# State times weight in two heads: 64-row tiles on half the array each, in place of operands stacked over 128 rows

## The chip, the core and the metric

The kernel runs on one core of a Trainium2 chip. The metric is the device time of one execution in microseconds (us), the median of several runs. The core's engines are TensorE (PE, with its weight loads as PEld), VectorE (DVE), ScalarE (ACT), GpSimd (POOL) and SyncE (SP), which issues all the DMAs here. Each runs its own instructions in order and waits for the others by semaphores.

## The reference

Eight batches of eight heads: `x` is 512 x 64 per head, `state` 32 x 64. Attention is run in both directions, and the result goes through two gated products (d_model 512, d_ff 1536).

```python
scores = scale * np.matmul(x, state.transpose(0, 1, 3, 2))
a = softmax(scores)
xread = np.matmul(a, state)
scores2 = scale * np.matmul(state, x.transpose(0, 1, 3, 2))
a2 = softmax(scores2)
sread = np.matmul(a2, x)
attn = np.concatenate([xread, sread], axis=2)
...
h = attn @ moe_w_a * (attn @ moe_w_b) @ moe_w_out
g = h @ moe2_w_gate
out = (g * sigmoid(g) * (h @ moe2_w_val)) @ moe2_w_out
```

`softmax` stands here for the lines that subtract the maximum, exponentiate and divide; the last lines are the bodies of two functions. The weights come as 64-bit numbers and are turned into 32-bit ones on the chip.

## The kernel before, in words

For the rows that come from `xread`, `attn @ w` is `a @ (state @ w)`: the kernel multiplies each head's state by the 64 rows of the weight that belong to that head, and the attention weights `a` then take the place of the activations. This product, **state @ w**, is the place of the change. It is made for q = 0, 1 (batches 0 to 3 and 4 to 7, whose four states of 32 rows make the 128 columns of one left operand), for fp = 0 to 5 (512 columns of both first weights) and for eight heads.

Every product is made in a 32-bit format with a shortened mantissa (fp32r). A number is split into a high part, the cast (`copy` on ACT), and a low part, the rest (`subtract` on DVE), and a product of two split numbers is a few matmuls that are summed in a PSUM bank. `convert` makes a 32-bit weight `cv_w` of 128 rows, that is the rows of heads 2p and 2p + 1, by steps on ACT, DVE and POOL. `stacked` (L415) splits it so that for each head h the buffer `w[:, h]` holds the head's high part over its own 64 partitions and its low part over the other 64: two casts (L420) and two subtractions (L336, called for the low parts) over 64 partitions each. The state is laid out twice, over partitions 0 to 63 and again over 64 to 127, and split by `states` into `st_hi` and `st_lo`.

`state_w` (L441) takes one `w` and makes the two heads one after the other. For a head it takes one PSUM bank (tag `pt`) and issues two matmuls over all 128 rows: `st_hi` by the stack (L450), which sums high x high and high x low, and `st_lo` by the stack (L451). `sw_out` copies the bank to `swo` (L328 on ACT or L330 on DVE) and writes it to a tensor in DRAM, from which `sw` later reads `swr` and splits it into `swh` and `swl` for the main product `p` (L652). For q = fp = 0 the copies go straight to the first `swr`.

There are two banks with the tag `pt`; scores (`psc`, `pr`), transposes (`pat`, `pa`, `pst`), the attention product `psr` and the states' products `sw` share them. The main products use the other banks.

The order on all engines is written by a planner before anything runs. Each task has engines it may run on, an estimated cost (`PASS_US` for a matmul of 512 columns), a due time `by` and perhaps a start. `Program.order` hands out, engine by engine, the due task that fits, provided that its buffers (`w`, `h` and the two `pt` banks) are free in the planner's own count; the engines then keep that order. A pool of spare tasks, `warm` (L901, two small matmuls each), fills PE's gaps in the start. Each weight tile is converted, split and multiplied with the state of q = 0; the products with q = 1 are listed after the four tiles of an fp and come due later.

After the first products (p, po, about 700 us) come those of the second layer (pA to pD, pu); the change touches none of them.

Of the kernel before, what the change touches and what calls it, by code (L numbers as in the profile page):

```python
# [10 lines left out]
F32 = mybir.dt.float32  # L11
# [7 lines left out]
P = 128  # L19
# [30 lines left out]
DUE = (-8.0, 12.0, 29.0, -17.0, 92.0, 4.0)  # L50
# [15 lines left out]

ACT_US, DVE_US, FAST_US, POOL_US = ((0.09, 0.84e-3), (0.07, 1.05e-3), (0.07, 0.53e-3), (0.2, 2.6e-3))
PASS_US, HALF_PASS_US = 0.2267, 0.12
HOP_US, PE_HOP_US = 0.25, 0.3
DMA_US, DMA_ISSUE_US, DMA_BYTES_PER_US = 2.2, 0.5, 3.6e5  # L70

# [3 lines left out]
def act(n):  # L75
    return {"ACT": ACT_US[0] + ACT_US[1] * n}


def dve(n, fast=False):
    a, b = FAST_US if fast else DVE_US  # L80
    return {"DVE": a + b * n}
# [176 lines left out]
class Kernel:  # L258
# [151 lines left out]
        self.hi_lo(raw, lambda: raw.t, hi, lambda: hi.t, lo, lambda: lo.t, 1024)  # L410
        return hi, lo

    def stacked(self, name, src_buf, src, **kw):

        nc = self.nc  # L415
        w = self.w_buf(name)
        for h in range(2):
            own, oth = slice(64 * h, 64 * h + 64), slice(64 - 64 * h, 128 - 64 * h)
            self.p.add(
                act(512), lambda e, own=own, h=h: nc.scalar.copy(w.t[own, h], src()[own]), [src_buf], [(w, (h, 0))],  # L420
                **kw
            )
            self.subtract(
                lambda oth=oth, h=h: w.t[oth, h], lambda own=own: src()[own],
                lambda own=own, h=h: w.t[own, h].bitcast(F32), dve(512), [src_buf, (w, (h, 0))], [(w, (h, 1))], **kw
            )
        return w

    def sw_out(self, ps, d, dst, name, by, here=None):

        o = self.h_buf(name)
        self.copy(lambda: o.t, lambda: ps.t, 512, [ps], [o], by=by + 2)
        if here is not None:
            raw, head = here
            r = 32 * (head % 4)
            self.dma(
                lambda: raw.t[r:r + 32, head // 4], lambda: o.t[::4], [o], [(raw, head)], 32 * 2048, by=by + 3
            )
        self.dma(lambda: dst(d.t), lambda: o.t, [o], [(d, name)], P * 2048, by=by + 5)

    def state_w(self, st, fp, p, w, q, by):  # L441

        hi, lo = st
        for h in range(2):
            head = 2 * p + h
            c = slice(head * P, (head + 1) * P)
            ps = self.bank(f"sw{q}_{fp}_{head}")

            def fn(pe, ps=ps, h=h, c=c):
                pe.matmul(ps.t, lhsT=hi.t[:, c], rhs=w.t[:, h], start=True, stop=False)  # L450
                pe.matmul(ps.t, lhsT=lo.t[:, c], rhs=w.t[:, h], start=False, stop=True)  # L451

            self.pe(2 * PASS_US, fn, [hi, lo, (w, (h, 0)), (w, (h, 1))], [ps], by=by)
            r = 32 * (head % 4)
            self.sw_out(
                ps, self.sw_d[q, fp], lambda t, head=head, r=r: t[:, head // 4, r:r + 32].rearrange("b n c -> n b c"), f"swo{q}_{fp}_{head}", by,
                (self.sw_first, head) if q == fp == 0 else None
            )

# [432 lines left out]
    def body(self):  # L892
        nc, p = self.nc, self.p
# [23 lines left out]
        begin, t = {}, FIRST_US  # L917
# [6 lines left out]
        def made(f):  # L924

            return begin[0, f]
# [4 lines left out]
        for fp in range(NFP):  # L931
            t0 = made(2 * fp)
            late = []
            for k in range(KD):
                nm = f"w1_{fp}_{k}"
                t, f = self.convert(self.wab[0][fp, k], nm, by=t0 - DUE[0], start=max(0, t0 - LEAD[0]))
                d = self.wf[fp, k]
                self.dma(lambda d=d: d.t, f, [(t, 0)], [d], P * 2048, by=t0 + 30)
                w = self.stacked(nm, (t, 0), f, by=t0 - DUE[0] + 2)
                self.state_w(st[0], fp, k, w, 0, t0 - DUE[0] + 4)  # L940
                late.append((st[1], fp, k, w, 1, t0 + DUE[1] + 3 * k))
            for a in late:
                self.state_w(*a)
            for f in (2 * fp, 2 * fp + 1):
                wo1[f] = self.weight(self.wo[0][f], f"wo1_{f}", by=begin[0, f] + DUE[2], start=max(0, begin[0, f] - LEAD[1]))
        ws, sw, xs_s = {}, {}, []
        for blk, lo, hi in order:
            self.stretch = STRETCH[0] if blk in range(4) else STRETCH[1]
            t0 = self.clock = max(self.clock, begin[blk, lo])
# [7 lines left out]
            if blk == "s":  # L957
# [14 lines left out]
                xb, n = xs_s, ST  # L972
            else:
# [4 lines left out]
                xb, n = xs[blk], T  # L978
# [18 lines left out]
        for u in range(0, B, 2):  # L997
            ops = self.operands(u, u + 1, self.clock - 30)
            xs_s = []
            if u == B - 2:  # L1000
                d = self.x2["s"]
                for k in range(KD):
# [3 lines left out]
                        start=self.clock - 10  # L1006
# [58 lines left out]
```

## Time and profile before

| | |
|---|---|
| median of 3 runs | 1496.96 us (1496.48 to 1498.74) |
| span of the profiled execution | 1495.1 us; its own time beside that is not listed |
| PE busy, modelled | 1486.0 us, 7016 matmuls |
| DVE, ACT, POOL busy | 1050.2, 648.3, 102.1 us |
| granted clock | 1.000 of full |
| state @ w on PE | 192 matmuls, from 22.9 to 312.9 us |

The span runs from the first to the last instruction. "Busy" on PE counts a matmul from its start to a modelled end, so overlapping ones count once, and short gaps are covered; the distance from one start to the next tells more. In the timeline, a length with a count covers a merged run. Weight loads (PEld) overlap the matmul before them.

### The profile page before, as it was taken

The numbers are of one execution on the slowest core, as the hardware profiler recorded it, in microseconds if no ns is written. First come the engines' busy times: TensorE is split into PE (matmuls) and PEld (weight loads), VectorE is DVE, ScalarE is ACT, GpSimd is POOL, SyncE is SP. The second block draws the span as 40 slices with busy tenths as digits, with TensorE's granted clock in tenths as the row PEclk, the third lists the DMA queues.
The fourth block names the chain that finished last, engine by engine and source line by source line (L and its number), as shares of the span: only waits on it lengthen the run. The fifth ranks groups of instructions, "written<-read, shape, count | busy, mean of one in ns | idle before, by whom it ended". The sixth has DMA issues, their size and how long they took to land.

```text
span 1495.1 us, 19610 instructions
## 1 busy us (share of the span) xinstructions
PE 1486.0 (99%) x7016; PEld 1241.0 (83%) x7016; DVE 1050.2 (70%) x1786; ACT 648.3 (43%) x1152; POOL 102.1 (7%) x78
## 2 busy tenths in 40 slices
PE   9999999999999999999999999999999999999998
PEld 8777888788888888998888888888888888888887
DVE  7999758756787778776777996466855577545554
ACT  7777656644556566655333432222323133222220
POOL 1212102100011111110000100000000000000000
PEclk9999999999999999999999999999999999999999
DMA  8765644744455466666947886355664446433412
GB/s 318 274 243 200 232 181 158 260 155 145 171 202 200 169 244 224 243 227 245 386 172 250 305 317 252 138 188 198 244 234 164 140 183 232 169 112 129 155 57 71
DMA packets 111185, 305.90 MB, mean 205 GB/s; under 512 B 11760, under 2 KB 12784, under 8 KB 111088
## 3 DMA queue, kind: packets, MB, share of 16 engines
q1 hardware_dynamic: 111088, 304.66, 56.8%
q8 instruction: 55, 0.90, 0.2%
q14 instruction: 42, 0.34, 0.1%
HBM read 223.35 MB, written 80.74 MB: 203 GB/s over the span
## 4 chain that ended last, share of the span: by engine, by line
PE 96%; ACT 1%; DVE 1%; DMA 1%; issue 1%; SPq 0%; ACTq 0%; DVEq 0%
PE pu L851 17%; PE p L652 17%; PE po L687 17%; PE pC L757 9%; PE pB L757 9%; PE pA L757 9%; PE pD L757 4%; PE p_s L652 2%; PE psr L612 2%; PE psc L503 1%; PE sw L450 1%; PE sw L451 1%; PE pvs L652 1%; PE po_s L687 1%; PE pgs L652 1%; PE pus L851 1%
## 5 line engine op out<-in xcount | busy, mean ns | idle before, releaser
L687 PE MATMUL po<-hs,wo 128*128 128x512 f32 x1152 | 287.3, 393 | 0.0
L687 PEld LDWEIGHTS po<-hs,wo 128*128 128x128 f32 x1152 | 215.1, 188 | 45.1 <-issue 1.4
L652 PE MATMUL p<-xs,swh 128*128 128x512 f32 x768 | 238.3, 391 | 0.0
L652 PEld LDWEIGHTS p<-xs,swh 128*128 128x128 f32 x768 | 143.3, 188 | 29.7 <-issue 0.5
L652 PE MATMUL p<-xs,swl 128*128 128x512 f32 x384 | 149.6, 390 | 0.0
L757 PE MATMUL pB<-x,w 128*128 128x512 f32 x576 | 146.2, 389 | 0.0
L757 PE MATMUL pA<-x,wg 128*128 128x512 f32 x576 | 146.2, 389 | 0.0
L851 PE MATMUL pu<-wo,hv 128*128 128x512 f32 x576 | 140.6, 389 | 0.0
L851 PE MATMUL pu<-wo,hu 128*128 128x512 f32 x576 | 138.5, 389 | 0.0
L757 PEld LDWEIGHTS pA<-x,wg 128*128 128x128 f32 x576 | 108.1, 188 | 22.4
L757 PEld LDWEIGHTS pB<-x,w 128*128 128x128 f32 x576 | 108.1, 188 | 22.4
L851 PEld LDWEIGHTS pu<-wo,hu 128*128 128x128 f32 x576 | 107.9, 188 | 22.2
L851 PEld LDWEIGHTS pu<-wo,hv 128*128 128x128 f32 x576 | 107.9, 188 | 22.2
L771 DVE TENSOR_TENSOR t<-c,pB 128x512 f32<-128x512 f32 x96 | 65.7, 685 | 82.3 <-PE pB L757 80.4
L671 DVE TENSOR_TENSOR a<-a,p 128x512 f32<-128x512 f32 x96 | 65.7, 684 | 70.5 <-PE p L652 57.6
L775 ACT ACTIVATE av<-t 128x512 f32<-128x512 f32 x48 | 30.3, 632 | 176.4 <-DVE t L771 173.2
L328 ACT COPY a<-p 128x512 f32<-128x512 f32 x87 | 51.0, 586 | 91.2 <-PE p L652 84.6
L343 ACT CAST hs<-a 128x512 fp32r<-128x512 f32 x96 | 59.8, 622 | 62.0 <-DVE a L671 52.4
L652 PEld LDWEIGHTS p<-xs,swl 128*128 128x128 f32 x384 | 72.1, 188 | 15.2
L869 DVE TENSOR_TENSOR part<-part,pu 128x512 f32<-128x512 f32 x64 | 43.7, 684 | 47.8 <-PE pu L851 47.6
L336 DVE TENSOR_TENSOR hs<-a,hs 128x512 fp32r<-128x512 f32 x96 | 69.0, 719 | 11.2 <-ACT hs L343 10.4
L757 PE MATMUL pC<-x,wv 128*128 128x512 f32 x288 | 73.1, 389 | 0.0
(180 smaller groups left out, 2365.7 us busy)
## 6 DMA issues: line engine op xcount, KB each, us to landing
w<-w SPq DMA_DIRECT2D x120, 512.0 KB, 4.9
sw<-swo SPq DMA_DIRECT2D x96, 256.0 KB, 2.8
wg<-w2g SPq DMA_DIRECT2D x48, 512.0 KB, 4.7
wv<-w2v SPq DMA_DIRECT2D x48, 512.0 KB, 4.8
wo<-w2o SPq DMA_DIRECT2D x48, 512.0 KB, 6.0
swr<-sw SPq DMA_DIRECT2D x47, 512.0 KB, 4.9
raw_w<-in_wab SPq DMA_DIRECT2D x24, 512.0 KB, 7.1
xt<-in_xt SPq DMA_DIRECT2D x32, 256.0 KB, 5.0
```

What stands on the lines that cost most here:

```text
L328: self.nc.scalar.copy(out(), in_())
L336: lambda e: self.by_engine[e].tensor_tensor(out=out(), in0=in0(), in1=in1(), op=ALU.subtract), r, w, **kw
L343: self.p.add(act(n), lambda e: self.nc.scalar.copy(hi(), src()), [src_buf], [hb], **kw)
L612: pe.matmul(ps.t[:, :256], lhsT=a2.t[:, l], rhs=xn.t[:, r], start=c == 0, stop=c == 3)
L652: pe.matmul(ps.t[:, :n], lhsT=l, rhs=r, start=i == 0, stop=i == last)
L671: self.vec(n, lambda v, a=a, pb=pb: v.tensor_tensor(out=a.t[:, :n], in0=a.t[:, :n], in1=pb.t[:, :n], op=ALU.mult), [pb], [a])
L687: pe.matmul(ps.t[:, :n], lhsT=wo[f].t[:, hw, c], rhs=hs.t[:, hh, :n], start=st, stop=sp)
L757: pe.matmul(ps.t, lhsT=w.t[:, hw, c], rhs=x.t[:, hx], start=start and i == n == 0, stop=stop and i == 1 and n == 2, skip_group_check=True)
L771: self.vec(512, lambda e: e.tensor_tensor(out=out.t, in0=ta(), in1=tb(), op=op), [a, b], [out])
L775: p.add(act(n), lambda e: nc.scalar.activation(out=a.t[:, :n], in_=g.t[:, :n], func=AF.Sigmoid), [g], [a])
L851: pe.matmul(ps.t, lhsT=h.t[:, hh, c], rhs=wo[f].t[:, hw], start=f == steps[0] and i == 0, stop=f == steps[-1] and i == 2)
L869: self.vec(w, lambda v: v.tensor_tensor(out=to(), in0=part.t[:, j % 2, :w], in1=ps.t[:, :w], op=ALU.add), [ps, (part, j)], [ok], by=by)
```

## The change

`stacked` goes. A weight is split plainly, by `hi_lo`: one cast over 128 rows to `w[:, 0]` and one subtraction to `w[:, 1]`. `state_w` takes both banks at once and issues six matmuls as one task: high x high, high x low and low x high, and in each of the three first the head of partitions 0 to 63, then that of 64 to 127, each reading 64 rows of `lhsT` and `rhs`, and writing its own bank. The product low x low, which the stack brought along, is no longer made. The task costs the planner `3 * PASS_US + SWITCH_US` in place of two tasks of `2 * PASS_US`; `SWITCH_US` is a number for the order alone.

```diff
+SWITCH_US = 0.25
...
-    def stacked(self, name, src_buf, src, **kw):
-
-        nc = self.nc
-        w = self.w_buf(name)
-        for h in range(2):
-            own, oth = slice(64 * h, 64 * h + 64), slice(64 - 64 * h, 128 - 64 * h)
-            self.p.add(
-                act(512), lambda e, own=own, h=h: nc.scalar.copy(w.t[own, h], src()[own]), [src_buf], [(w, (h, 0))],
-                **kw
-            )
-            self.subtract(
-                lambda oth=oth, h=h: w.t[oth, h], lambda own=own: src()[own],
-                lambda own=own, h=h: w.t[own, h].bitcast(F32), dve(512), [src_buf, (w, (h, 0))], [(w, (h, 1))], **kw
-            )
-        return w
...
     def state_w(self, st, fp, p, w, q, by):
 
         hi, lo = st
+        ps = [self.bank(f"sw{q}_{fp}_{2 * p + h}") for h in range(2)]
+
+        def fn(pe):
+            for n, (l, k) in enumerate(((hi, 0), (hi, 1), (lo, 0))):
+                for h in range(2):
+                    rows, c = slice(64 * h, 64 * h + 64), slice((2 * p + h) * P, (2 * p + h + 1) * P)
+                    pe.matmul(ps[h].t, lhsT=l.t[rows, c], rhs=w.t[rows, k], start=n == 0, stop=n == 2)
+
+        self.pe(3 * PASS_US + SWITCH_US, fn, [hi, lo, w], ps, by=by)
         for h in range(2):
             head = 2 * p + h
-            c = slice(head * P, (head + 1) * P)
-            ps = self.bank(f"sw{q}_{fp}_{head}")
-
-            def fn(pe, ps=ps, h=h, c=c):
-                pe.matmul(ps.t, lhsT=hi.t[:, c], rhs=w.t[:, h], start=True, stop=False)
-                pe.matmul(ps.t, lhsT=lo.t[:, c], rhs=w.t[:, h], start=False, stop=True)
-
-            self.pe(2 * PASS_US, fn, [hi, lo, (w, (h, 0)), (w, (h, 1))], [ps], by=by)
...
-                ps, self.sw_d[q, fp], lambda t, head=head, r=r: t[:, head // 4, r:r + 32].rearrange("b n c -> n b c"), f"swo{q}_{fp}_{head}", by,
+                ps[h], self.sw_d[q, fp], lambda t, head=head, r=r: t[:, head // 4, r:r + 32].rearrange("b n c -> n b c"), f"swo{q}_{fp}_{head}", by,
...
-                w = self.stacked(nm, (t, 0), f, by=t0 - DUE[0] + 2)
+                w = self.w_buf(nm)
+                self.hi_lo(
+                    (t, 0), f, w, lambda w=w: w.t[:, 0], w, lambda w=w: w.t[:, 1], 512, by=t0 - DUE[0] + 2
+                )
```

With other tasks the planner writes another order, from the first state @ w on. Names below are buffers: `sw_0_6` is the bank of fp 0, head 6; the number behind it tells buffers of one name apart; `x2` counts equal instructions. Line numbers have moved: L336 and L330 are L337 and L331 after the change, L652 and L687 are L638 and L673.

First place: PE in the start, from heads 6 and 7 of the first weights, before:

```order
L450 MATMUL sw_0_6_329<-w_0_3_255,st_hi 128x512
L451 MATMUL sw_0_6_329<-w_0_3_255,st_lo 128x512
L901 MATMUL warm<-ident 128x128 x4
L450 MATMUL sw_0_7_346<-w_0_3_255,st_hi 128x512
L451 MATMUL sw_0_7_346<-w_0_3_255,st_lo 128x512
L567 MATMUL pat_0_352<-ident,sn_0_116 128x128 x4
L901 MATMUL warm<-ident 128x128 x4
L567 MATMUL pat_1_374<-ident,sn_1_152 128x128 x4
```

and after, where the same two heads stand:

```order
L503 MATMUL pr_1_415<-strt_118,xt_1_0_361 128x128
L503 MATMUL pr_1_415<-strt_118,xt_1_1_366 128x128
L489 MATMUL psc_1_427<-xt_1_0_361,strt_118 128x512
L489 MATMUL psc_1_427<-xt_1_1_366,strt_118 128x512
L887 MATMUL warm<-ident 128x128 x6
L435 MATMUL sw_0_6_453<-w_0_3_254,st_hi 128x512
L435 MATMUL sw_0_7_454<-w_0_3_254,st_hi 128x512
```

Heads 6 and 7 have moved behind block 0's transposes `pat` and behind block 1's scores `pr` and `psc`, which stood after them.

Second place: DVE in the start, at the low parts of the first four weights, before:

```order
L330 COPY sT_0_237<-psc_0_202 128x512
L336 TENSOR_TENSOR w_0_0_166<-cv_w_0_0_104,w_0_0_166 64x512 x2
L336 TENSOR_TENSOR w_0_1_210<-cv_w_0_1_134,w_0_1_210 64x512 x2
L336 TENSOR_TENSOR w_0_2_222<-cv_w_0_2_148,w_0_2_222 64x512 x2
L336 TENSOR_TENSOR w_0_3_255<-cv_w_0_3_154,w_0_3_255 64x512 x2
L330 COPY swo_0_4_313<-sw_0_4_304 128x512
```

and after:

```order
L331 COPY sT_0_237<-psc_0_201 128x512
L337 TENSOR_TENSOR w_0_0_166<-cv_w_0_0_104,w_0_0_166 128x512
L337 TENSOR_TENSOR w_0_1_209<-cv_w_0_1_134,w_0_1_209 128x512
L337 TENSOR_TENSOR w_0_2_221<-cv_w_0_2_148,w_0_2_221 128x512
L337 TENSOR_TENSOR w_0_3_254<-cv_w_0_3_154,w_0_3_254 128x512
L331 COPY swo_0_1_282<-sw_0_1_262 128x512
```

Eight subtractions have become four, and DVE's first copy out of a bank is that of head 1 now, not of head 4.

Third place: PE in the steady stretch, at the fourth weights (fp 3), before:

```order
L687 MATMUL po_3_3_1601<-hs_3_1_1489,wo_1_750 128x512 x3
L450 MATMUL sw_3_0_1708<-w_3_0_1496,st_hi 128x512
L451 MATMUL sw_3_0_1708<-w_3_0_1496,st_lo 128x512
L450 MATMUL sw_3_1_1712<-w_3_0_1496,st_hi 128x512
L451 MATMUL sw_3_1_1712<-w_3_0_1496,st_lo 128x512
L687 MATMUL po_3_0_1552<-hs_3_2_1614,wo_2_816 128x512 x3
L450 MATMUL sw_3_2_1726<-w_3_1_1536,st_hi 128x512
```

and after (the two `st_hi` rows of a head read halves 0 and 1 of `w`):

```order
L673 MATMUL po_3_3_1603<-hs_3_1_1498,wo_1_650 128x512 x3
L435 MATMUL sw_3_0_1725<-w_3_0_1484,st_hi 128x512
L435 MATMUL sw_3_1_1726<-w_3_0_1484,st_hi 128x512
L435 MATMUL sw_3_0_1725<-w_3_0_1484,st_hi 128x512
L435 MATMUL sw_3_1_1726<-w_3_0_1484,st_hi 128x512
L435 MATMUL sw_3_0_1725<-w_3_0_1484,st_lo 128x512
L435 MATMUL sw_3_1_1726<-w_3_0_1484,st_lo 128x512
L673 MATMUL po_3_0_1564<-hs_3_2_1591,wo_2_741 128x512 x3
L673 MATMUL po_3_1_1574<-hs_3_2_1591,wo_2_741 128x512 x3
L435 MATMUL sw_3_2_1758<-w_3_1_1519,st_hi 128x512
```

Runs of four, with three `po` steps between some of them, have become runs of six with six steps between them.

## Rows read from the trace of the kernel before

**Rows 1.** the page: span, busy time of each engine, one group (count, busy, mean ns).

```profile
span 1495.1 us, 19610 instructions
...
PE 1486.0 (99%) x7016; PEld 1241.0 (83%) x7016; DVE 1050.2 (70%) x1786; ACT 648.3 (43%) x1152; POOL 102.1 (7%) x78
...
L687 PEld LDWEIGHTS po<-hs,wo 128*128 128x128 f32 x1152 | 215.1, 188 | 45.1 <-issue 1.4
```

**Rows 2.** busy time by stage; columns: length, PE, PEld, DVE, ACT, POOL busy, granted clock, DMA.

```profile
0.00:40.00 40.00, 37.38 (x249) 32.71 (x250) 29.76 (x55) 28.62 (x48) 6.92 (x10) 1.00 0.84 318
40.00:320.00 280.00, 278.02 (x1242) 223.87 (x1241) 225.27 (x395) 187.78 (x340) 45.12 (x32) 1.00 0.61 216
```

**Rows 3.** timeline of PE: start, length, line, operation, tiles, shape, count.

```profile
164.29 0.39 PE L450 MATMUL sw<-w,st_hi 128*128 128x512 f32 x1
...
165.19 0.62 PE L652 MATMUL p<-xs,swh 128*128 128x512 f32 x2
```

**Rows 4.** the chain of waits: start and length of runs of matmuls, in us.

```profile
209.00 2.72 PE p L652 x12
...
640.24 2.88 PE p_s L652 x24
```

**Rows 5.** timeline of PE: after a wait for a bank, and around a transpose.

```profile
61.02 0.50 PE L450 MATMUL sw<-w,st_hi 128*128 128x512 f32 x1 [0.27 <-ACT swo L328]
61.36 0.40 PE L451 MATMUL sw<-w,st_lo 128*128 128x512 f32 x1
...
130.04 0.38 PE L623 MATMUL pst<-ident,sr 128*128 128x128 f32 x2
130.17 0.71 PE L652 MATMUL p<-xs,swh 128*128 128x512 f32 x2
130.72 0.40 PE L652 MATMUL p<-xs,swl 128*128 128x512 f32 x1
```

**Rows 6.** waits of PE's weight loads: total us, times, longest.

```profile
PEld sw L450 <- ACT swo L328: 5.6, 14, 1.2
...
PEld sw L450 <- DVE swo L330: 1.8, 4, 0.7
```

**Rows 7.** the splits of state weights, then of other weights: ns min/median/max.

```profile
L420 ACT CAST w<-cv_w x48: 602/618/657, 14.4 to 259.0; 64x512 fp32r<-64x512 f32 x48
L336 DVE TENSOR_TENSOR w<-cv_w,w x48: 678/686/1669, 21.3 to 264.4; 64x512 fp32r<-64x512 f32 x48
...
L343 ACT CAST w<-c x24: 611/621/630, 403.8 to 843.3; 128x512 fp32r<-128x512 f32 x24
L336 DVE TENSOR_TENSOR w<-c,w x24: 672/683/693, 405.2 to 844.8; 128x512 fp32r<-128x512 f32 x24
```

**Rows 8.** timeline of PE from the first state @ w to 70 us.

```profile
22.92 0.48 PE L450 MATMUL sw<-w,st_hi 128*128 128x512 f32 x1
...
38.77 0.71 PE L652 MATMUL p<-xs,swh 128*128 128x512 f32 x2
...
54.11 0.71 PE L652 MATMUL p<-xs,swh 128*128 128x512 f32 x2
...
65.30 1.96 PE L687 MATMUL po<-hs,wo 128*128 128x512 f32 x6
...
69.38 5.60 PE L687 MATMUL po<-hs,wo 128*128 128x512 f32 x24
```

**Rows 9.** timeline of ACT, then of DVE, in the start.

```profile
13.80 0.67 ACT L376 ACTIVATE cv_w<-raw_w 128x512 int32<-128x512 uint32 x1
14.37 1.23 ACT L420 CAST w<-cv_w 64x512 fp32r<-64x512 f32 x2
...
35.88 1.05 ACT L343 CAST swh<-swr 128x1024 fp32r<-128x1024 f32 x1 [0.35 <-DMA swr<-swo]
...
21.25 6.08 DVE L336 TENSOR_TENSOR w<-cv_w,w 64x512 fp32r<-64x512 f32 x8
...
30.92 0.69 DVE L330 COPY swo<-sw 128x512 f32<-128x512 f32 x1
```

## The prediction, made before the changed kernel ran

> **What bounds the kernel now.** I read the page first: PE is busy for 1486.0 of 1495.1 us [rows 1]. PE's busy time is modelled, so I went on to the steps. In the chain of waits a run of twelve p matmuls takes 2.72 us [rows 4], 0.227 us a step, and after the first 70 us the steps keep that pace, apart from a few waits. The granted clock is 1.00 in the stages shown, the 2.4 GHz level [rows 2]. So the time is PE's steps, plus the start, in which PE runs fillers, plus waits. DVE is busy for 225 of 280 us between 40 and 320 us, ACT for 188 [rows 2]: close to full in the start, but not what later steps wait for. What the change saves on DVE and ACT can count only in the start and in waits; what it does to PE counts nearly in full.
>
> The state matmuls are the place of the change. A pair of heads is four steps, st_hi and st_lo for each, from 164.29 to 165.19 us [rows 3]: 0.907 by 4 x 0.227. There are 2 x 6 x 4 = 48 pairs, 192 steps.
>
> **PE: the price of a pair.** Now a pair is six matmuls over 64 rows, alternating between the upper and the lower half of the array; each still loads its own weights and streams 512 columns. No row of before has a matmul over 64 rows, so the price is bounded from the nearest.
> - *Lower end, 0.68 us:* the two halves run abreast, three steps of 0.227.
> - *Without any price for the switch, but with the loads in line:* in the p_s run 24 loads with matmuls of 256 columns take 2.88 us [rows 4], so a load and its matmul can follow the next at 0.12 us. Six loads then start their matmuls 0.12 apart, and the last takes a whole step: 5 x 0.12 + 0.227 = 0.827.
> - *Upper end, 1.53:* at both switches (whole array to halves, and back) PE must run empty and load uncovered. A matmul's record is 0.39 long where the step is 0.227 [rows 3], so emptying costs 0.16; a load takes 0.188 [rows 1] and is hidden in the step before it now. 0.827 + 2 x (0.16 + 0.19) = 1.53.
>
> Two rows lie nearest to a switch. Around a transpose the operands' format changes twice: 130.04 to 130.72 us holds two transposes and two steps [rows 5], 0.68 us, where two steps are 0.454 and the two transposes some 0.2 at 0.11 each: almost no price. After a wait for a bank, where PE has run empty, the next step comes 0.34 later (61.02 to 61.36 [rows 5]) and not 0.227: 0.113 for filling up again. A change of rows should be nearer to the second, but on the way in the upper half's matmul may start while the lower half still empties. I take 0.113 once for each run of six: 0.827 + 0.113 = **0.94 us a pair**, 0.033 above now.
>
> The Trainium skill speaks against me on one side. "TensorEngine Tiling (Array Packing)", section Key Properties, says that changing the tiling mode, not just the tile, drains the engine; no run here shows it yet. By that rule a pair is nearer to the drain rival below.
>
> **PE: how many pairs count.** 47 runs of six come out of the new order for 48 pairs, since the steady stretches put three or six other steps between them (third piece). Where PE runs fillers a pair costs nothing. By my walk through the start, 7 pairs lie there, 5 (and one that is late) between it and 69 us, 36 after that: 36 x 0.033 = **+1.2 us**.
>
> **DVE and ACT.** A weight was two casts over 64 rows at 0.618 us and two subtractions at 0.686; the 128-row forms on other weights take 0.621 and 0.683 [rows 7]. For 24 weights that removes 24 x 0.62 = 15 us on ACT and 24 x 0.69 = 16 us on DVE. After 70 us I cost this at nothing: PE hides it, its waits there being for banks. The copies out of the banks stay 96, but now 52 on ACT and 44 on DVE. DMA issues stay as many, a pair's two behind each other. POOL's 24 additions keep their order. SP issues block 1's x loads behind the copies of heads 2 and 3, some us earlier or later; I put that into the start's error.
>
> **Banks.** A pair now needs both banks before its first step. Before, each bank had three po steps and the other head's two steps, 0.68 + 0.45 = 1.13 us, to be emptied; now, with six steps between runs, 1.36. So I leave the waits as they are: 18 weight loads waited 7.4 us in all, many of them in the start [rows 6]. What queues behind a waiting pair on PE is the main p or po step, in order.
>
> **The start.** Here the order moves most. The four low halves run on DVE from 21.25 for 6.08 us [rows 9], 0.76 each; at 0.68 they end near 24.0 and not 27.3. That gain is lost: ACT's copy of the first bank now stands behind three conversions of 0.57 (step 13.80 to 14.37 [rows 9]), so the first two banks are empty near 24.9, the next two near 27.4; then the transposes of sn take both until DVE has split them, near 31.1. The third pair ends near 32.3; then block 1's pat, pr and psc take the banks, and DVE's copy of psc frees the last near 38.3. The pair of heads 6 and 7, the last that block 0 needs, runs near 38.5, and its copies end near 40.2, where the last one ended at 31.6 before [rows 9]. From there to the cast of swh it was 3.9 us by DMA (35.88 less 0.35 [rows 9]); two splits follow, and a pair of the next weights stands ahead in PE's order. So the first p comes near 47.8 and not at 38.77 [rows 8].
>
> But SP, ACT and PE then have no gap: before, the stretch behind block 0's p held the second state's pairs and fillers until block 1's p at 54.11 [rows 8]. Now block 1's p follows at 47.8 + 24 x 0.227 = 53.2. From there to the long po run: 24 p steps (5.44), 12 po steps (2.72), a psc (1.3, up to 65.30 [rows 8]) and 5 pairs (4.7) make 67.4; with the one pair that before had run by then, 68.3, against 69.38 [rows 8]. **-1.1 us**, by a long walk with small errors, so +-3.
>
> **Sum.** +1.2 - 1.1 = +0.1. The profiled execution's span of 1495.1 lies 1.9 under the median of 1496.96, with what lies around it; that stays. **Forecast: 1497 us, no change**; its own range, with the start's +-3, is 1493 to 1501. With a pair at p us the sum is -1.1 + 36 x (p - 0.907) + 6 x (p - 0.94). A measurement of this kernel can tell about 0.2%, 3 us, from no change.
>
> **Rivals.**
> - *The switch drains PE* (slower). Emptying at both ends alone makes 0.827 + 2 x 0.16 = 1.15: +9 us, 1506. With a load of 0.12 uncovered at each end, 1.39: +19, 1516. It decides from p = 1.0 on. For it: nothing in before changes rows, so nothing shows that it is cheap. Against it: the change of format in rows 5 is nearly free. This is the skill's rule as a mechanism here. Chance 0.28.
> - *Switches free* (faster). p = 0.827 gives -4.7, 1492; abreast at 0.68 gives -11, 1486. For it: rows 5's transposes, and the loads' pace of 0.12. "TensorE: Matmul & The Clock Gate" of the Trainium skill, Part 3 (Packing small matmuls), has matmuls in different row groups start about 4 ns apart, which would be the 0.68; no run here shows it yet. Chance 0.20.
> - *The halves do not overlap*, so that the change does not do what it says: six whole steps, 1.36 us, +18, 1515. Against it: nothing but the way the tiles are laid. Chance 0.07.
> - *Both banks at once become the wait*: if half of the 36 late runs wait 0.41 us (7.4 / 18 [rows 6]) more, +7, 1504. Against it: 1.36 us between runs. Chance 0.05.
>
> **Numbers.** Forecast 0.40, rivals 0.60. The range 1489 to 1513 leaves out the fully abreast end and the costliest drains, some 2 in 10. Faster by over 0.2%: 0.20 from the free switch and 0.03 from the start, 0.23. Slower: 0.28 + 0.07 + 0.05, and 0.02 of the start, 0.42. Within: 0.35.
>
> **What will show it.** In the steady timeline, from a run's first state matmul to the next p or po step: 0.94 by me, 0.68 to 0.83 if free, 1.15 or more if it drains, 1.36 if there is no overlap. In the start: the first p near 47.8, block 1's p near 53. In PE's waits: sw no more often than 18 loads. I am wrong if the time moves by more than 3 us with p between 0.86 and 1.0: then the start or the banks did it.

## The result, and the profile after

The changed kernel takes 1508.11 us (median of 4 runs, 1507.55 to 1510.67), the kernel before beside it 1497.2 us: ratio 1.0076, 95% interval 1.0061 to 1.0090. It is **10.9 us slower**. Forecast was no change, 1497 us; that is missed by more than the 3 us which the prediction called the least that can be told. The time lies inside the range of 1489 to 1513, which was wide enough to take in a price for the switch, and on the side of the rivals that make it slower.

The profiled execution of the changed kernel is the slowest of the four, 1510.67 us. In it the first loads landed some 2.2 us later than in the one shown of before (first scores at 10.05 us for 8.03, first state @ w at 25.34 for 22.92 [rows 8]). These 2.2 us belong to that execution and not to the change: the orders differ only from the first state @ w on, and in the traces of the other runs the first scores come anywhere from 6.96 to 9.85 us.

The page of the changed kernel, the lines that answer to [rows 1]:

```profile
span 1508.9 us, 19755 instructions
...
PE 1498.2 (99%) x7112; PEld 1230.9 (82%) x7112; DVE 1048.8 (70%) x1792; ACT 621.7 (41%) x1098; POOL 102.7 (7%) x78
...
L673 PEld LDWEIGHTS po<-hs,wo 128*128 128x128 f32 x1152 | 213.2, 188 | 52.6 <-issue 10.5
```

PE is as full as before. The third line is the first sign: `po` is the same 1152 loads, but PE's loads stood 52.6 us ahead of them where it was 45.1, and 10.5 of that by "issue" where it was 1.4. The engine had nothing to wait for that the profile shows, and yet did not load. The waits of PE's weight loads (total us, times, longest), as [rows 6]:

```profile
PEld po L673 <- issue: 10.5, 30, 0.4
PEld sw L435 <- issue: 8.5, 24, 0.4
PEld p L638 <- issue: 5.8, 16, 0.7
...
PEld sw L435 <- ACT swo L329: 2.6, 6, 0.9
...
PEld sw L435 <- DVE xs L337: 1.3, 1, 1.3
```

The first three lines are the two ends of the runs of 64-row tiles, some 0.36 us each. Before, `po` had 6 such waits, `p` had 2 and `sw` none. Of the 47 runs, 26 are followed by a waiting `po` load and 13 by a waiting `p` load of these lines (the rest of the two lines stands behind scores, as before); the others are followed by fillers, by scores, or by a `p` load that is put down to an engine. Of the runs' beginnings 24 are put down to "issue", and most of the others, equally long, to whichever engine came last. So it is with four of the six loads that the view puts down to `swo`, 0.36 each. What is left of the waits for a bank, 7.4 us in 18 loads before, are two loads at one pair, 0.94 and 0.21, beside one for `xs`, all in the start.

Timeline of PE at a steady pair, as [rows 3]:

```profile
182.01 0.84 PE L673 MATMUL po<-hs,wo 128*128 128x512 f32 x3
182.79 0.73 PE L435 MATMUL sw<-w,st_hi 64*128 64x512 f32 x4
183.36 0.40 PE L435 MATMUL sw<-w,st_lo 64*128 64x512 f32 x2
183.68 2.33 PE L673 MATMUL po<-hs,wo 128*128 128x512 f32 x9
```

Here the price of a pair can be read. Three `po` steps begin at 182.01, so the next ordinary step would begin at 182.69; the tiles begin at 182.79. Six matmuls then take 0.90 us to the next `po`. In the records their starts lie at 182.787 and 182.790, 183.122 and 183.125, 183.357 and 183.360. The two halves run abreast, **three slots and not six**. But the first slot is 0.335 long and not 0.232, the last step of the run is followed after 0.324 and not 0.227, and the first `po` behind it after 0.337. The nine `po` are 2.33 us long, where nine ordinary steps are 8 x 0.227 + 0.39 = 2.21. From the last step before the run to the second step behind it are 0.319 + 0.897 + 0.337 = 1.55 us; without two ordinary steps of 0.227 a pair costs **1.10 us**, 0.19 above the 0.907 of before. That is 0.68 for three slots and 0.42 for two changes, some 0.2 each: 0.09 ahead of the change and 0.11 behind it. I read them as PE running empty and filling again, since the 0.11 is that of a step after a wait (61.02 to 61.36 [rows 5]). But a load, 0.188 [rows 1], that is no longer hidden would come to nearly the same sum, and no run here separates the two.

Busy time by stage, as [rows 2], with the stretch in which the clock fell (columns: length, PE, PEld, DVE, ACT, POOL busy, granted clock, DMA):

```profile
40.00:320.00 280.00, 277.59 (x1283) 205.33 (x1283) 220.42 (x392) 163.41 (x288) 44.52 (x32) 0.99 0.61 211
51.40:58.20 6.80, 6.67 (x17) 4.75 (x18) 3.93 (x7) 2.80 (x6) 1.59 (x1) 0.50 1.01 318
```

DVE and ACT are relieved as forecast (220 us for 225, 163 for 188 between 40 and 320 us). From 51.4 to 58.2 us PE had half its clock, the 1.2 GHz level, where [rows 2] show it at full.

Timeline of PE in the start, as [rows 8]; the entry in brackets is an idle time and what ended it:

```profile
25.34 0.74 PE L435 MATMUL sw<-w,st_hi 64*128 64x512 f32 x4
...
38.92 1.83 PE L503 MATMUL pr<-strt,xt 128*128 128x128 f32 x14 [0.66 <-DMA xt<-in_xt]
...
43.74 0.73 PE L435 MATMUL sw<-w,st_hi 64*128 64x512 f32 x4
...
48.59 0.49 PE L435 MATMUL sw<-w,st_hi 64*128 64x512 f32 x1
50.06 0.73 PE L435 MATMUL sw<-w,st_hi 64*128 64x512 f32 x3 [0.98 <-DVE xs L337]
...
51.53 1.70 PE L435 MATMUL sw<-w,st_hi 64*128 64x512 f32 x4 [0.50 <-ACT swo L329]
...
53.59 1.22 PE L638 MATMUL p<-xs,swh 128*128 128x512 f32 x2
...
58.38 0.40 PE L638 MATMUL p<-xs,swl 128*128 128x512 f32 x1
...
61.34 0.62 PE L638 MATMUL p<-xs,swh 128*128 128x512 f32 x2
```

The first p step comes at 53.59 (38.77 before), and block 1's first, 24 steps on, at 61.34 (54.11 before). PE stood empty before 50.06 and before 51.53; then the clock fell. The 11 steps from 53.59 to 58.38 take 4.79 us, 0.435 each; the 13 from there to 61.34 take 0.228 each.

ACT and then DVE in the start, as [rows 9]:

```profile
49.70 1.05 ACT L344 CAST swh<-swr 128x1024 fp32r<-128x1024 f32 x1
50.89 1.07 ACT L329 COPY swo<-sw 128x512 f32<-128x512 f32 x2
```

```profile
23.38 2.98 DVE L337 TENSOR_TENSOR w<-cv_w,w 128x512 fp32r<-128x512 f32 x4
```

The low halves of the first four weights take 2.98 us, 0.75 each, for 6.08 before. The bank that the pair at 51.53 waits for is copied at 50.89, behind the cast of `swh`.

The splits of the 24 state weights, as [rows 7], and the last state matmul:

```profile
L344 ACT CAST w<-cv_w x24: 601/620/667, 16.6 to 273.0; 128x512 fp32r<-128x512 f32 x24
L337 DVE TENSOR_TENSOR w<-cv_w,w x24: 630/682/1174, 23.4 to 273.7; 128x512 fp32r<-128x512 f32 x24
```

```profile
L435 PE MATMUL sw<-w,st_lo x96: 385/393/626, 25.9 to 325.7; 64*128 64x512 f32 x96
```

The last state matmul starts at 325.7, where it was 312.9. At equal progress (the same number of other steps issued, a pair in hand on one side counted at 0.907 us) the two executions are 2.2 us apart after the first loads, 8.4 at 93 us of before, 13.0 from 321 us on, and 13.8 at the end. So the start costs 8.4 - 2.2 = **6.2 us** (five pairs at 0.19 among it), the 36 pairs behind it **4.5 us** net, and the rest, 0.9, comes in the second layer, where PE has one late wait. The three make 11.6 in this pair of executions, and the medians lie 10.9 apart.

```profile
PE pC L743 <- DVE c L757: 0.4, 1, 0.4
```

### The profile page after: what moved, and what is told of

The parts are those of the page before. It is cut to its first block, busy times and chain, and to the rows that moved or that the text cites. A ratio compares the mean times of both kernels' runs of the same rounds, so it can differ in the third digit from the quotient of the medians.

```text
span 1508.9 us, 19755 instructions
## 1 busy us (share of the span) xinstructions
PE 1498.2 (99%) x7112; PEld 1230.9 (82%) x7112; DVE 1048.8 (70%) x1792; ACT 621.7 (41%) x1098; POOL 102.7 (7%) x78
## 4 chain that ended last, share of the span: by engine, by line
PE 95%; DVE 2%; DMA 1%; issue 0%; SPq 0%; POOL 0%; ACT 0%; POOLq 0%; DVEq 0%; ACTq 0%
PE p L638 17%; PE po L673 17%; PE pu L837 17%; PE pC L743 9%; PE pA L743 8%; PE pB L743 8%; PE pD L743 4%; PE sw L435 3%; PE p_s L638 2%; PE psr L598 2%; PE psc L489 2%; PE pvs L638 1%; PE po_s L673 1%; PE pgs L638 1%; PE pus L837 1%; DMA xt<-in_xt 1%
## 5 line engine op out<-in xcount | busy, mean ns | idle before, releaser
L673 PE MATMUL po<-hs,wo 128*128 128x512 f32 x1152 | 288.8, 395 | 0.0
L673 PEld LDWEIGHTS po<-hs,wo 128*128 128x128 f32 x1152 | 213.2, 188 | 52.6 <-issue 10.5
L638 PE MATMUL p<-xs,swh 128*128 128x512 f32 x768 | 242.2, 397 | 0.1
L638 PEld LDWEIGHTS p<-xs,swh 128*128 128x128 f32 x768 | 143.2, 189 | 36.0 <-issue 5.8
L638 PE MATMUL p<-xs,swl 128*128 128x512 f32 x384 | 150.4, 392 | 0.0
L329 ACT COPY a<-p 128x512 f32<-128x512 f32 x79 | 46.3, 586 | 102.5 <-PE p L638 97.9
L638 PEld LDWEIGHTS p<-xs,swl 128*128 128x128 f32 x384 | 72.7, 189 | 15.5
L337 DVE TENSOR_TENSOR hs<-a,hs 128x512 fp32r<-128x512 f32 x96 | 67.7, 706 | 9.4 <-ACT hs L344 8.8
```

Source lines behind the costliest of these rows:

```text
L329: self.nc.scalar.copy(out(), in_())
L337: lambda e: self.by_engine[e].tensor_tensor(out=out(), in0=in0(), in1=in1(), op=ALU.subtract), r, w, **kw
L638: pe.matmul(ps.t[:, :n], lhsT=l, rhs=r, start=i == 0, stop=i == last)
L673: pe.matmul(ps.t[:, :n], lhsT=wo[f].t[:, hw, c], rhs=hs.t[:, hh, :n], start=st, stop=sp)
```

## The experiments

Two theories stood for the loss. *Switch:* each run of tiles costs a fixed 0.19 us more than the stacked matmuls did. *Start:* the pair, which wants both `pt` banks at once, is pushed back by tasks that want one, and the first p comes late. The runs of before beside the experiments had medians of 1497.45 to 1498.63 us; each ratio goes against those of its own chip.

### The two parts apart: late, first

`late` uses the tiles for fp 1 to 5 alone and keeps the stack and the single heads for fp 0; `first` does the reverse.

```diff
+TILED = lambda fp: fp > 0     # late; first: fp == 0
...
+        if not TILED(fp):
+            return self.state_w_whole(st, fp, p, w, q, by)
...
-                w = self.w_buf(nm)
-                self.hi_lo(
+                if TILED(fp):
+                    w = self.w_buf(nm)
+                    self.hi_lo(
...
+                else:
+                    w = self.stacked(nm, (t, 0), f, by=t0 - DUE[0] + 2)
```

> Heads in 64-row tiles for fp 1 to 5 alone; for fp 0 the weights are stacked and the heads multiplied one by one, as before. Switch theory (a run of six costs 1.10 us on PE in place of 0.907, because the array empties and fills again at both ends): 40 pairs x 0.19 = +7.6, less the 2 to 3 us of bank waits that the change did away with, so 1501 to 1503 against 1497 before; the start is that of before, with the first p near 39 us. Start theory (the loss is all in the start): 1497. In the trace each run of six again takes 0.89 to 0.90 us from its first matmul to the next main step.

> 64-row tiles for fp 0 alone; fp 1 to 5 stacked as before. Start theory (the order of the start costs some 6 us, with a fallen clock after 51 us): 1502 to 1504 against 1497, the first p near 53 us. Switch theory alone: only the pairs of fp 0 that PE's fillers don't hide, fewer than 3 of 8, pay 0.19, so 1497 to 1498.

`late`: 1500.91 us, ratio 1.0023 (1.0014 to 1.0032), +3.4 us. `first`: 1503.09 us, ratio 1.0035 (1.0022 to 1.0048), +5.6 us. Together 9.0 of the 10.9; `late` came out 0.1 us under the span that was given for it. In `late` the first p comes as before and the ends of the tiles are there (timeline of PE, then waits of the weight loads):

```profile
39.00 0.70 PE L676 MATMUL p<-xs,swh 128*128 128x512 f32 x2
```

```profile
PEld po L711 <- issue: 10.2, 29, 0.4
PEld sw L454 <- issue: 8.5, 24, 0.4
```

In `first` the loss is in the start, with the first p at 56.47 us and the clock halved once more (busy time by stage):

```profile
51.50:58.30 6.80, 6.21 (x14) 3.77 (x15) 4.97 (x7) 3.86 (x6) 0.86 (x1) 0.50 0.82 276
```

So both theories hold, each for its part. Some loss in the start is there without the clock's fall, too: a fall as above makes the mean granted clock 0.998, the five runs of `first` have means of 0.997 to 1.000, and the two at 1.000 and 0.999 took 1503.09 and 1500.45 us, the other three 1502.36 to 1505.01.

### A planner that keeps banks for the pair: queue

One rule is added to `Program.order`: once a due task is held back for want of `pt` banks, no later task on that engine may take one. The order of the kernel before is not changed by this rule, since each of its tasks takes one bank: where one is held for want of a bank, a later one finds none either.

```diff
                 held = []
+                stuck = False
...
+                    if "pt" in need:
+                        if stuck or room["pt"] < need["pt"]:
+                            stuck = True
+                            held.append(item)
+                            continue
```

> The changed kernel with one rule more in the planner: while a due task waits for PSUM banks, a later one may not take a bank. Starvation theory (a pair needs both banks at once, and single-bank tasks that are due later kept taking the one that came free): the pair of heads 6 and 7 comes before block 1's scores again, the first p near 41 to 44 us, no fall of the clock, and the time falls by 4 to 6 us to 1502 to 1504. If the start is bound by the weights' conversion on ACT and DVE, not by banks: 1508, no change.

1502.65 us, ratio 1.0033 (1.0021 to 1.0045), +5.1 us: 5.8 of the 10.9 come back. Timeline of PE:

```profile
40.30 0.50 PE L441 MATMUL sw<-w,st_hi 64*128 64x512 f32 x1
40.97 0.74 PE L441 MATMUL sw<-w,st_hi 64*128 64x512 f32 x3 [0.16 <-DVE xs L343]
...
42.78 0.70 PE L644 MATMUL p<-xs,swh 128*128 128x512 f32 x2
...
50.70 0.73 PE L644 MATMUL p<-xs,swh 128*128 128x512 f32 x2
```

The first p comes at 42.78 and block 1's at 50.70, PE stands empty before the pair ahead of the first p for 0.16 us only, and the clock stays at full. At equal progress the kernel is 0.7 us behind before at 93 us and 5.2 at 321 us. In the changed kernel the start's loss came from the starving pair; what is left goes with the tiles.

### Both heads as one task, without tiles: pairtask, queue_pair

`pairtask` is the kernel before with the two heads of a weight in one task that takes both banks; `queue_pair` adds the rule of `queue`.

```diff
+        ps = [self.bank(f"sw{q}_{fp}_{2 * p + h}") for h in range(2)]
+
+        def fn(pe):
+            for h in range(2):
+                c = slice((2 * p + h) * P, (2 * p + h + 1) * P)
+                for n, l in enumerate((hi, lo)):
+                    pe.matmul(ps[h].t, lhsT=l.t[:, c], rhs=w.t[:, h], start=n == 0, stop=n == 1)
+
+        self.pe(4 * PASS_US, fn, [hi, lo, w], ps, by=by)
```

> The kernel before (stacked weights, whole-array matmuls) with both heads of a weight as one task that takes both banks at once: no change of tiles anywhere. Starvation theory: the start is late as in the changed kernel, the first p near 48 to 53 us, +4 to +6 there, and the steady stretch gains the 2 to 3 us of bank waits: 1498 to 1501. If taking both banks is harmless and only the switch of tiles costs: 1494 to 1497.

> Stacked weights and whole-array matmuls, both heads as one task, with the planner's rule on banks: no change of tiles and no starvation. If both theories hold, the start is that of before within 1 us and the steady stretch keeps the regained bank waits: 1494 to 1497 against 1497. If the rule on banks costs as much as it gives: 1498.

`pairtask`: 1498.45 us, ratio 1.0007 (0.9998 to 1.0016). Its first p comes at 47.65, but at equal progress it is only 2.0 us behind before at 93 us, not the 4 to 6 that were expected, and 1.4 at 321 us. So a late first p by itself doesn't cost what the changed kernel's start costs. `queue_pair`: 1497.32 us, ratio 0.9997 (0.9988 to 1.0006), level with before and 0.3 us above the expected span. Waits of its weight loads:

```profile
PEld sw L456 <- ACT swo L334: 3.7, 11, 0.7
PEld sw L456 <- DVE xs L342: 3.6, 2, 2.6
```

The second line holds one long wait in the start (timeline of PE, then busy time by stage):

```profile
51.97 0.50 PE L456 MATMUL sw<-w,st_hi 128*128 128x512 f32 x1 [2.20 <-DVE xs L342]
```

```profile
50.00:60.00 10.00, 7.76 (x33) 5.96 (x33) 9.72 (x15) 6.50 (x12) 1.73 (x1) 1.00 0.89 296
```

PE stood empty for 2.20 us there, and the clock stayed at full.

`queue_pair` differs from `queue` in nothing but tiles for stack and what the planner makes of that, and stands 5.3 us below it (5.7 where each is taken against before on its own chip). At equal progress `queue_pair` is 2.6 us behind before at 93 us, no better than `pairtask` although its first p comes at 43.11, and level from 321 us on; `queue` goes from 0.7 to 5.2. Over the 36 pairs between, the tiles thus cost 4.5 + 2.6 = 7.1 us more, **0.197 a pair** with what differs in waits, for the 0.19 read from the timeline.

### Is it the ends of a run? queue_apart, double

`queue_apart` issues the same six matmuls head after head; `double` issues the six twice in a run.

```diff
-            for n, (l, k) in enumerate(((hi, 0), (hi, 1), (lo, 0))):
-                for h in range(2):
+            for h in range(2):                                            # queue_apart
+                for n, (l, k) in enumerate(((hi, 0), (hi, 1), (lo, 0))):
...
+            for n, (l, k) in 2 * [*enumerate(((hi, 0), (hi, 1), (lo, 0)))]:   # double
```

> As the run with the planner's rule on banks, but the six matmuls of a pair head after head (three over partitions 0 to 63, then three over 64 to 127) and not alternating. Abreast theory (matmuls start in order, and two start together only where they stand next to each other on different halves): the first of the second head starts with the last of the first head, five slots of 0.227 and not three, 1.35 us from the first matmul to the next main step in place of 0.90, and 1502.7 + 41 x 0.45 = 1521. No overlap at all: six slots, 1.58 us and 1531. If the order within a run does not matter: 0.90 us and 1503.

> As the run with the planner's rule on banks, but each pair's six matmuls are issued twice in a row (the second time starts the sums anew), twelve in a run. Switch theory (a fixed price at each end of a run, and 0.227 for two matmuls between): 0.90 + 0.68 = 1.58 us from the first matmul to the next main step, with the same 0.32 before the run and 0.34 after its first main step. If matmuls over 64 rows are simply slower (1.10 / 3 = 0.37 for two): 1.10 + 0.90 = 2.0 us.

`queue_apart`: 1503.52 us, ratio 1.0042 (1.0027 to 1.0057), as `queue`. Of the three cases expected it is the one in which the order within a run does not matter. Timeline of PE:

```profile
105.39 0.74 PE L441 MATMUL sw<-w,st_hi 64*128 64x512 f32 x4
105.96 0.40 PE L441 MATMUL sw<-w,st_lo 64*128 64x512 f32 x2
106.28 0.96 PE L679 MATMUL po<-hs,wo 128*128 128x512 f32 x3
```

The program has two `st_hi`, one `st_lo`, and again two and one; the timeline, in order of start, merges four `st_hi` and then two `st_lo`. The run takes 0.89 us still. The second head's first matmul, issued fourth, starts 0.010 us behind the first: so alternating the halves in the program is not what makes them run abreast.

`double`: 1534.59 us (one run). Timeline of PE at a run of twelve:

```profile
107.44 0.73 PE L441 MATMUL sw<-w,st_hi 64*128 64x512 f32 x4
108.01 0.39 PE L441 MATMUL sw<-w,st_lo 64*128 64x512 f32 x2
108.24 0.62 PE L441 MATMUL sw<-w,st_hi 64*128 64x512 f32 x4
108.70 0.39 PE L441 MATMUL sw<-w,st_lo 64*128 64x512 f32 x2
109.02 0.73 PE L644 MATMUL p<-xs,swh 128*128 128x512 f32 x2
```

Twelve matmuls take 1.58 us to the next p, six took 0.895: three slots more are 0.69, 0.23 each, and no more is lost. The ends stay 0.318 and 0.337. The 0.42 us is paid per run, not per matmul, and the time agrees: 48 x 0.69 = 33 us, and it stands 31.9 above `queue`.

### Tiles for the start alone, with the rule: queue_first, best

`queue_first` is `first` with the rule of `queue`. `best` takes both heads as one task in the stacked fp 1 to 5 too.

> 64-row tiles for fp 0 alone, stacked weights for fp 1 to 5, with the planner's rule on banks. Both theories: the start no later than before (the switches there lie beside PE's fillers), the rest as before: 1496 to 1499, against 1503 without the rule. If the plain split's saving on ACT and DVE shortens the start: 1494 to 1496.

> Tiles for the first 512 columns (fp = 0) alone, whole-array stacked matmuls for the other five, there both heads as one task as in queue_pair, and the planner's rule of queue. If the start and the late stretch add up piece by piece, the start stands some 2 us better than in queue_pair (which was level with before) and nothing is paid for tiles later: 1495 to 1496 us, about 0.1% under before. If each order brings waits of its own, as queue_first did, it comes out level with before, 1497 to 1498.

`queue_first`: 1498.0 us, ratio 1.0009 (0.9999 to 1.0019); of the 5.6 us that `first` lost nearly all is back. `best`: 1497.9 us beside 1498.63, ratio 0.9998 (0.9989 to 1.0007), level with before and not the 0.1% below that was hoped for. Waits of PE in `best`:

```profile
PE sw L480 <- ACT swo L336: 2.2, 2, 1.3
```

At equal progress it is 0.6 us behind before at 71 us and 1.6 at 93 us, where `queue_pair` is 1.8 and 2.6. The two waits for a bank that its order has at 145 and 186 us, 2.2 us, put it 4.0 behind; at 321 us it is 2.0 behind, and `queue_pair` level. So the start is some 1 us better than in `queue_pair`, and the order's own waits take more than that back. Its profiled execution is 0.9 us above the median of its runs. No version ran that beats the kernel before.

### More fillers, and the planner's price: warm60, queue_price

`warm60` is the changed kernel with `WARM` at 60 for 44, so that PE doesn't stand empty before the clock falls. `queue_price` is `queue` with `SWITCH_US` at 0.42 for 0.25, the price as measured.

> The changed kernel with 60 spare tasks for PE in place of 44; in the new order ten more small matmuls stand before the pair that waited for its banks at 49 to 51.5 us, and more between the first p steps. Clock theory (PE stood empty there, and the granted clock then fell to half from 51.4 to 58.2 us): the clock stays at 1.0 throughout, and the time falls by the 3 us that some 15 steps at 0.43 in place of 0.23 cost, to 1505, while the late start itself stays. If the clock's fall has another cause: it falls again, and 1508.

> The changed kernel with the planner's rule on banks, and the price of a run in its table set to what the trace shows (3 x 0.2267 + 0.42 = 1.10 and not 0.93). If the planner's wrong price put things into a bad order: 1500 to 1501 against 1502.7. If the switches themselves are what is left: 1502 to 1503.

`warm60`: 1512.41 us, ratio 1.0101 (1.0085 to 1.0116), above both times that were expected. Busy time by stage, then fillers in the timeline of PE:

```profile
0.00:65.00 65.00, 62.79 (x407) 50.81 (x408) 49.98 (x90) 35.90 (x61) 15.52 (x16) 1.00 0.74 268
```

```profile
147.22 1.16 PE L887 MATMUL warm<-ident 128*128 128x128 f32 x8
...
149.09 0.61 PE L887 MATMUL warm<-ident 128*128 128x128 f32 x4
...
158.83 2.05 PE L887 MATMUL warm<-ident 128*128 128x128 f32 x16
...
162.38 0.71 PE L887 MATMUL warm<-ident 128*128 128x128 f32 x4
```

The clock stays at full and the first p comes at 50.86, but at 93 us the kernel is still 5.6 us behind, and then 32 of the 64 new filler matmuls stand between main steps, where the planner still had them. What the fall of the clock cost by itself was not isolated.

`queue_price`: 1506.31 us, ratio 1.0057 (1.0044 to 1.0069), worse than with the wrong price and outside both spans expected. Waits of PE:

```profile
PE sw L441 <- ACT swo L335: 1.3, 3, 0.7
...
PE sw L441 <- DVE xs L343: 0.9, 1, 0.9
PE sw L441 <- DVE swo L337: 0.5, 1, 0.5
```

It has 2.7 us of waits before `sw`, where `queue` has 1.0. That is 1.7 of the 3.7 us between them; where the rest went stays open. The planner's count of PE is now right, but the order that comes out is not better for it: an order's waits change with any of its numbers.

## Why the prediction was right or wrong

The time came out inside the range, but no change had been forecast, and the mechanism behind that forecast was wrong in two terms, the switch and the start. Both errors raise the time; the range held because it was wide.

- **The price of a pair, 0.94 us: wrong, 1.10.** The bounds held. Both halves of the sum missed. The slots were too dear: 0.827 for loads in line, where the halves run abreast at 0.68. The change of rows was far too cheap: one refill of 0.113, where each of the two changes costs 0.09 ahead of it and 0.11 behind it, 0.42 in all. The step that failed is the sentence that the upper half's matmul may start while the lower half still empties, with the transposes of [rows 5] as the nearest row. They change the format of operands and not the rows of the array, and the price of the one says nothing of the other. The rule of "TensorEngine Tiling (Array Packing)" in the Trainium skill, section Key Properties, that changing the mode drains the engine, agrees with this trace: the loads at both ends of a run stand back by some 0.36 us (the three "issue" lines above). "TensorE: Matmul & The Clock Gate" in the Trainium skill, Part 3, has matmuls of different row groups start about 4 ns apart, and the trace agrees: 3 to 4 ns here. Both rules held, and I had set each as a rival to the other; the price is their sum.
- **47 runs, 36 late pairs: right in number.** At 0.19 the 36 make 36 x 0.19 = 6.8 us in place of 1.2.
- **Banks, left as they were: wrong, in the good direction.** The forecast put many of the 18 waiting loads into the start; in the trace of before 11 of them, 4.9 of the 7.4 us, stand behind 70 us. After the change no state load waits for a bank there (one `psc` does, 0.8 us), and the late pairs cost 4.5 us net and not 6.8. That a pair leaves six steps to empty the banks was in the forecast; I didn't draw the gain from it.
- **The start, -1.1 +- 3: wrong, +6.2.** The first p came at 53.59 for 47.8. Of the 5.8 us, 2.2 are this execution's loads and 0.66 the wait for block 1's `xt`. Three pairs, not one, stand between heads 6 and 7 (43.74) and the first p; PE stands 1.5 us at two of them; and the last of them, at half the clock and with a short wait for its second bank, takes 2.06 us for 0.9. Then I had block 0's p steps at 0.227, and they took 7.75 us for 5.45. The walk held the clock to be given, and it added up each engine's own work without the gaps that the engines leave each other. `queue` shows that the loss comes from the order. The clock's share of it is open: by these rows the last pair took 1.2 and the first 11 p steps 2.3 us more than at full clock, but `warm60` kept the clock at full and was 5.6 us behind at 93 us, with more fillers in the start, and `first` lost 5.6 us in a run with a mean clock of 1.000.
- **DVE and ACT: right.** 0.620 and 0.682 us at 128 rows, 24 of each, and no gain behind 70 us.
- **The rivals.** The drain came true, as far as the records tell the emptying from the load. That 1.10 lies near its lower price of 1.15 is in part luck: it had 0.15 too much for the slots and 0.1 too little for the two ends. With 1.10 in the forecast's own sum the time would be 1504; the rest is the start, less what the bank waits gave. Free switches, halves that do not overlap and a new wait for banks did not. The last condition, time off by more than 3 us with p between 0.86 and 1.0, was not met: p was outside it, and the start was off too.

## What to carry to other kernels

A switch between whole-array and tiled matmuls costs some 0.2 us at each end, 0.42 us a run here; with three slots in the place of four, 0.23 us are saved, so by these numbers tiles would pay only in runs that save at least two slots, or where tiled runs can stand next to each other. That is an estimate from the price of a run; no version here has a case that pays. A task that wants two buffers at once can be starved by tasks that want one, where a planner serves whoever fits: protecting it gave back 5.8 us here in the tiled kernel, and 1.1 us, no more than the spread of the runs, in the one with whole-array pairs. And in a kernel that is bound by one engine in an order written beforehand, compare at equal progress: it separates the start, the steady price and the waits, which a total mixes.

## What the runs showed of the hardware

- Matmuls in the two halves of the array can start out of their order in the program: in `queue_apart` the fourth of six starts 0.010 us behind the first. The Trainium skill, "TensorE: Matmul & The Clock Gate", Part 3, has matmuls start in program order; this trace says otherwise, and the measurement decides.
- A switch costs the same 0.318 and 0.337 us beside `p` and `po` steps, whether six or twelve matmuls stand between.
- The granted clock fell to 0.50, the 1.2 GHz level, from 51.4 to 58.2 us in the changed kernel and from 51.5 to 58.3 in `first`. In the changed kernel PE had run one matmul between 48.06 and 50.06 us besides transposes, and stood empty again before 51.53. With a pause of 0.16 us in `queue` it did not fall, nor with one of 2.20 us in `queue_pair`, so an empty PE does not bring it down every time. What decides stays open.
